# Sliding-window attention with an expert layer on one core: the inner tiles' global transposes set right behind the local ones, and global probabilities issued behind local ones

## The chip, the cores and the metric

The kernel runs on one NeuronCore of a Trainium2 chip. The metric is the time of one execution in device microseconds (us); the median of several runs counts. Engines are named as in the profile: PE (TensorE, with PEld for its weight loads), DVE (VectorE), ACT (ScalarE), POOL (GpSimd) and SP (SyncE, which issues all DMAs here). Each engine takes its instructions in the order of its own queue and waits on semaphores of the others.

## The reference

```python
B, H, Sl, D = q_l.shape            # 8, 8, 512, 64; Sg = 32 global tokens
k_all = concat([k_g, k_l]); v_all = concat([v_g, v_l])
out_g = softmax(scale * q_g @ k_all.T) @ v_all          # global queries see every key
s_ll = where(abs(i - j) <= 32, scale * q_l @ k_l.T, -1e9)
out_l = softmax(concat([scale * q_l @ k_g.T, s_ll])) @ v_all
x = concat([out_g, out_l]) as 4608 tokens x 512
h = max(max(x @ w1, x @ w2), x @ w3)                    # 512 -> 768
return h @ w_out                                        # 768 -> 512
```

All in float32. Local queries see a window of 32 keys to either side and the 32 global keys; global queries see everything.

## The kernel before, in words

**Tiles and units.** Heads go in pairs: 8 batches x 4 pairs are 32 units, numbered p. The 512 local queries of a unit are cut into four tiles of 128, t = 0 to 3; tile number sl = 4p + t from tile 16 on (`ORDER` shuffles the first 16). A tile's window of keys is 192 or 224 wide. The two outer tiles of a unit (t = 0 and 3) are "mixed" from unit 8 on: their two heads' chunks of keys are packed into three blocks of 128 columns rather than four. "Inner" are t = 1 and 2.

**One pass of the main loop**, for tile sl, writes in this order: the transposes of tile sl + 1's probabilities (`trans`, L398, into the PSUM tile T; below this is the T group), some matmuls of the expert layer (`fill`), the scores of tile sl + 3 (`scores`, L367 into S), more `fill`, the product of tile sl with the values (`pv`, L464 into O), a piece of the next unit's global part, `fill`, the transpose of the global probabilities that go with tile sl + 1 (`transg`, L423 into S), `fill`, and loads and splits for later tiles. Nothing loops on the chip: all is written out. A scheduler then sets the order of each engine's queue from that text and the dependences; PE's queue follows the text closely, SP's is moved about.

**The expert layer** of batch b - 1 is a generator that `fill` draws from: 16 passes draw just the 288 matmul steps of one batch. From tile 32 on PE's gaps between attention steps are filled with it: L503 (x by w1, w2, w3) and L522 (by w_out), each with a moving width of 512 and accumulating in one of three PSUM buffers pm. Its first matmuls for a batch follow the T group of tile 33, 49, 65, 81, 97 or 113. Float32 is split into a high and a low part by a copy (L111 on ACT, L109 on DVE) and a subtraction (L103 on DVE or POOL), for q, k, v, the transposed probabilities pt, x and h alike.

**Local probabilities.** `scores` reduces and exponentiates a tile, POOL (or ACT or DVE) scales it by 1/sum (L124), and SP copies it from s into the tile prob (L385 for t = 1 and 2, L382 and L383 for the mixed ones), from which PE transposes.

**Global part of unit p.** In the passes with t = 0 and 1 of unit p - 1, `glob` computes the scores of the 64 global queries of two heads (L298, into S) and DVE and ACT bring them into sg, of which there is one buffer. In the pass with t = 2 `glob_soft` makes the softmax. From unit 8 on `glob_put` sends its six pieces (`GPUT`) from sg into the three blocks of probg: the pieces 0 and 3 (block 0) in that pass, the others (blocks 1 and 2) in the pass with t = 3. Piece 5 goes as two transfers (L338), the rest as one each (L335): seven issues, called puts below. A tile's global transpose takes one block: `GCH` gives block 0 to t = 0 and 2, block 1 to t = 1, block 2 to t = 3. For t = 3 it stands in the T group already (L401), for the others it is L423. From S it is cast into pt (ACT) and the rest subtracted (DVE). The tiles S (scores, global scores, global transposes) take turns in two PSUM buffers; T has one.

Of the kernel before, what the change touches and what calls it, by code (L numbers as in the profile page):

```python
# [21 lines left out]
NP = H // 2  # L22
# [36 lines left out]
def body(ctx, tc, kin, qin, vin, min_, win, out):  # L59
    nc = tc.nc  # L60
# [267 lines left out]
    def glob_put(p, which):  # L328
        if p >= B * NP:
            return  # L330
        s, g = pg[p][0], f32(pgt[p])
        for k in which:
            c0, n, i, h, d0 = GPUT[k]
            if k < 5 or p < 2 * NP:
                nc.sync.dma_start(out=g[64 * h:64 * h + 64, i, d0:d0 + n], in_=s[:, c0:c0 + n])  # L335
            else:
                for j in range(2):
                    nc.sync.dma_start(out=g[64:64 + SG, 2, 64 * j:64 * j + 64], in_=s[SG * j:SG * j + SG, 480:544])  # L338

    def scores(i):  # L340
        if i >= NS:
            return
        sl = ORDER[i]
        p, t = divmod(sl, 4)
        c0, n = WIN[t]

        ps = pm.tile([128, 512], F32, name="pm") if i < 8 else psS.tile([128, 512], F32, name="S")
        s = s4[:, i % 4]
        if i < EARLY:
            sc[i] = s  # L350
        else:
            if len(prob) < 2:
                prob.append(const.tile([128, 2, 256], F32R, name="prob", tag=f"prob{2 + len(prob)}"))
                pool.memset(f32(prob[-1]), 0.0)
            sc[i] = prob[i % 2]
        nm = small.tile([128, 2], F32, name="nm")
        z = small.tile([128, 2], F32, name="z")
        ze = z8[:, i % 4]
        ph = [ps[:, 0:224], ps[:, 224:448]]
        for j in range(2):  # L360
            if i in NATK:

                pe.matmul(ph[j][:, 0:n], lhsT=qraw[i][:, 128 * j:128 * j + 128], rhs=nat_k(p)[0][:, c0:c0 + n],  # L363
                          start=True, stop=True)
                continue
            for a in range(2):
                pe.matmul(ph[j][:, 0:n], lhsT=qs[i][:, a, 128 * j:128 * j + 128],  # L367
                          rhs=kst[p][:, j, c0:c0 + n], start=(a == 0), stop=(a == 1))
        for j in range(2):
            dve.tensor_tensor_reduce(out=s[:, j, 0:n], in0=ph[j][:, 0:n], in1=mask[:, (1, 0, 1, 0)[t], 32 * (t == 0):32 * (t == 0) + n],  # L370
                                     scale=-0.125, scalar=3.0e38, op0=ALU.add, op1=ALU.min, accum_out=nm[:, j:j + 1])
            act.activation(out=s[:, j, 0:n], in_=s[:, j, 0:n], func=AF.Exp, bias=nm[:, j:j + 1], scale=-1.0,  # L372
                           accum_out=ze[:, j, 0:1])
        dve.tensor_reduce(out=z, in_=ze, axis=AX.X, op=ALU.add)
        dve.reciprocal(out=z, in_=z)
        for j in range(2):
            times(s[:, j, 0:n], s[:, j, 0:n], z[:, j:j + 1])
        if i >= EARLY:
            d = f32(sc[i])
            if mixed(p, t):  # L380
                d = d.rearrange("p j x -> p (j x)")
                nc.sync.dma_start(out=d[:, 0:256].rearrange("p (j x) -> p j x", j=2), in_=s[:, :, 0:128])  # L382
                nc.sync.dma_start(out=d[:, 256:384].rearrange("p (j x) -> p j x", j=2), in_=s[:, :, 128:192])  # L383
            else:
                nc.sync.dma_start(out=d[:, :, 0:n], in_=s[:, :, 0:n])  # L385
        spend("d", 2 * (n * 1.04 + 220) + 440)
        spend("a", 2 * (n * 0.833 + 278))

    def trans(sl):
        if sl >= NS:  # L390
            return
        s = sc.pop(sl)
        ps = psT.tile([128, 512], F32, name="T")
        pr, one = (ps, ident) if sl < EARLY else (ps.bitcast(F32R), identr)
        m = 3 if mixed(*divmod(ORDER[sl], 4)) else 4
        s = s.rearrange("p j x -> p (j x)")
        for x in range(m):
            pe.transpose(pr[:, 128 * x:128 * x + 128], s[:, 128 * x:128 * x + 128], one)  # L398
        p, t = divmod(ORDER[sl], 4)
        if t == 3 and mixed(p, t):  # L400
            pe.transpose(pr[:, 384:512], pgt[p][:, 2], identr)  # L401
        src = ps.rearrange("p (x q) -> p x q", q=128)[:, 0:m]
        if sl < NAT:
            pt = pts[sl] = att.tile([128, 4, 160], F32, name="pt", tag="pt")
            copy(pt[:, 0:m, 0:128], src, True)
        else:
            pt = pts[sl] = att.tile([128, 4, 2, 160], F32R, name="pt", tag="pt")
            copy(pt[:, 0:m, 0, 0:128], src, True)
            sub(pt[:, 0:m, 1, 0:128], src, f32(pt)[:, 0:m, 0, 0:128], True)
        if t == 3 and mixed(p, t):  # L410
            transg(sl, ps[:, 384:512])

    def transg(sl, bank=None):
        if sl >= NS:
            return
        p, t = divmod(ORDER[sl], 4)
        if t == 3 and mixed(p, t) and bank is None:
            return
        pt = pts[sl]
        i, h, n = GCH[t]  # L420
        g = bank if bank is not None else psS.tile([128, 512], F32, name="S")
        if bank is None:
            pe.transpose((g if p < NP else g.bitcast(F32R))[:, 0:128], pgt[p][:, i], ident if p < NP else identr)  # L423
        if mixed(p, t):
            src = g[:, 0:SG + SG * n].rearrange("p (x g) -> p x g", g=SG)
            if sl < NAT:
                copy(pt[:, 0:n + 1, 128:160], src, True)
                return
            hi, lo = [pt[:, 0:n + 1, a, 128:160] for a in range(2)]
        else:  # L430
            src = g[:, 64 * h:64 * h + 64 * n].rearrange("p (c j g) -> p c j g", j=2, g=SG)
            if sl < NAT:
                copy(pt.rearrange("p (j c) q -> p c j q", c=2)[:, 0:n, :, 128:160], src, True)
                return
            v = pt.rearrange("p (j c) a q -> p c j a q", c=2)
            hi, lo = [v[:, 0:n, :, a, 128:160] for a in range(2)]
        copy(hi, src, True)
        sub(lo, src, f32(hi), True)
# [113 lines left out]
    def fill(n):  # L552
        if mm[0]:
            for _ in range(n):
                next(mm[0], None)
# [29 lines left out]
    for sl in range(NS):  # L585
        p, t = divmod(ORDER[sl], 4)
        b = p // NP
        settle(4500)
        if sl == 8:
            mm[0] = moe_local(0, 0, 256)  # L590
        elif sl == 16:
            mm[0] = chain(mm[0], moe_local(0, 256, 256))
        elif sl >= 32 and sl % 16 == 0:
            fill(400)
            mm[0] = moe_local(b - 1)
        n = (7, 6, 5, 9) if sl < 16 else (4, 4, 3, 7)
        trans(sl + 1)
        fill(n[0])
        next_scores(sl + 4 if sl < 12 else max(15, sl + 3))
        if sl >= 16:  # L600
            if t == 2:
                split_k(p + 2)
                load_k(p + 3)
        elif sl in (10, 14):
            load_k(sl // 4 + 2)
        elif sl == 15:
            load_k(6)
        fill(n[1])
        pv(sl)
        if sl < 8:  # L610
            if p < 3:
                if t == 0:
                    glob(p + 1, 0)
                    glob(p + 1, 1)
                else:
                    glob_soft(p + 1)
        elif sl < 16:
            if sl in (12, 13):
                glob(NP, sl - 12)
            elif sl == 14:  # L620
                glob_soft(NP)
        elif t <= 1:
            glob(p + 1, t)
        elif t == 2:
            glob_soft(p + 1)
            if p + 1 >= 2 * NP:
                glob_put(p + 1, (0, 3))
        elif p + 1 >= 2 * NP:
            glob_put(p + 1, (1, 2, 4, 5))
        fill(n[2])  # L630
        transg(sl + 1)
        fill(n[3])
        split_v(sl + 2)
        load_v(sl + 4)
        for _ in range(WS[sl] if sl < len(WS) else 0):
            weight_step()
        if sl < 8:
            if t == 1:
                xs.setdefault(0, []).append(split_x(xr[p][:, 0:2, 0:128]))
        elif sl < 16:  # L640
            if t == 3:
                split_x(xr[p][:, 2:4, 0:128], xs[0][p], 256)
        elif sl % 16 >= 12:
            q = b * NP + sl % 16 - 12
            xs.setdefault(b, []).append(split_x(xr[q][:, :, 0:128]))
# [60 lines left out]
```

## Time and profile before

| | |
|---|---|
| median of 3 runs | 834.85 us (832.93 to 837.02) |
| the profiled execution | 834.52 us, span 832.7 us, mean clock 0.994 |
| PE busy | 803.1 us (96%), 4620 matmuls |
| DVE, ACT, POOL busy | 511.4, 522.3, 513.2 us |
| DMA queue of SP | 93.56 MB, 37.2% of 16 engines |
| chain that ended last | PE 81% of the span |

How to read the rows: a timeline row is start in us from the span's beginning, duration, engine, line, operation, the program's names out<-in, shapes, and how many alike are merged (x4); in brackets the engine's idle time before it and what ended that. Matmuls are pipelined and their ends are modelled, so two rows of PE overlap; the time between two starts says more. A wait row is total time, number of waits and the longest. DMA rows on SP are the time of issuing; the landing is later.

### The profile page before, as it was taken

How to read it: one execution, taken by the hardware profiler on the slowest of the kernel's cores; microseconds unless marked ns; L12 is line 12 of the kernel's file. 1: busy time of each engine (PE TensorE's matmuls, PEld its weight loads, DVE VectorE, ACT ScalarE, POOL GpSimd, SP SyncE). 2: the span in 40 equal slices, each digit the busy share in tenths (PEclk: the TensorE clock that was granted, in tenths of full speed). 3: DMA queues.
4: the chain of work that ended last, by engine and by line, in shares of the span. 5: the costliest groups of instructions: out<-in, count | busy, mean ns of one | idle time of the engine just before them, and what ended most of it. 6: DMA issues, size and time to landing. Idle time of an engine off the chain costs nothing.

```text
span 832.7 us, 16036 instructions
## 1 busy us (share of the span) xinstructions
PE 803.1 (96%) x4620; PEld 680.7 (82%) x4620; DVE 511.4 (61%) x1789; ACT 522.3 (63%) x1495; POOL 513.2 (62%) x725
## 2 busy tenths in 40 slices
PE   7779899899999999999999999999999999999997
PEld 5469789878888888888888888878888888888896
DVE  3778744866776677766775766767666676411121
ACT  5788756777676767776676677776776666411111
POOL 4689836786677667867676676866776664311211
PEclk9999999999999999999999999999999999999999
DMA  7566544443344433343335333443335332100001
GB/s 251 174 221 221 186 148 122 132 133 110 110 115 129 117 104 112 100 149 104 103 106 165 111 96 102 125 127 99 105 93 165 115 86 57 59 13 0 26 26 26
DMA packets 106856, 94.58 MB, mean 114 GB/s; under 512 B 31888, under 2 KB 95248, under 8 KB 106768
## 3 DMA queue, kind: packets, MB, share of 16 engines
q1 hardware_dynamic: 106768, 93.56, 37.2%
q8 instruction: 37, 0.61, 0.3%
q14 instruction: 51, 0.42, 0.2%
HBM read 56.85 MB, written 8.91 MB: 79 GB/s over the span
## 4 chain that ended last, share of the span: by engine, by line
PE 81%; DVE 2%; DMA 1%; issue 1%; ACT 1%; POOL 1%; POOLq 0%; DVEq 0%; ACTq 0%
PE pm L503 48%; PE pm L522 15%; PE O L464 6%; PE S L367 5%; PE T L398 3%; PE S L298 2%; DMA prob<-s 1%; PE S L363 1%; PE O L457 1%; PE S L423 1%; ACT s L372 0%; DMA probg<-sg 0%; DVE s L370 0%; PE T L401 0%; DMA qraw<-q_in 0%
## 5 line engine op out<-in xcount | busy, mean ns | idle before, releaser
L503 PE MATMUL pm<-xs,wh 128*128 128x512 f32 (+1 forms) x1440 | 421.8, 368 | 5.5 <-ACT xs L111 2.4
L503 PEld LDWEIGHTS pm<-xs,wh 128*128 128x128 f32 x1440 | 253.3, 189 | 36.6 <-ACT xs L111 2.9
L503 PE MATMUL pm<-xs,wl 128*128 128x512 f32 (+1 forms) x720 | 264.1, 367 | 1.0 <-POOL wl L177 1.0
L503 PEld LDWEIGHTS pm<-xs,wl 128*128 128x128 f32 x720 | 136.3, 189 | 20.9 <-issue 1.6
L124 POOL TENSOR_SCALAR s<-s,z 128x224 f32<-128x224 f32 (+1 forms) x244 | 104.0, 438 | 67.7 <-ACT lox L111 38.7
L522 PE MATMUL pm<-woh,h 128*128 128x512 f32 x408 | 133.4, 398 | 0.9 <-POOL h L103 0.9
L372 ACT ACTIVATE s<-s,nm 128x224 f32<-128x224 f32 (+1 forms) x256 | 118.0, 462 | 19.2 <-DVE nm L370 18.0
L103 POOL TENSOR_TENSOR h<-m,h 128x512 fp32r<-128x512 f32 (+1 forms) x60 | 68.3, 1138 | 98.4 <-ACT h L111 98.2
L511 DVE TENSOR_TENSOR m<-pm,m 128x512 f32<-128x512 f32 (+1 forms) x120 | 72.9, 608 | 71.1 <-PE pm L503 70.7
L103 DVE TENSOR_TENSOR pt<-T,pt 128x512 fp32r<-128x512 f32 (+2 forms) x126 | 70.2, 557 | 72.1 <-ACT pt L111 71.7
L103 POOL TENSOR_TENSOR qs<-qraw,qs 128x256 fp32r<-128x256 f32 x100 | 73.0, 738 | 57.0 <-ACT qs L111 41.9
L370 DVE CUSTOM_DVE_ANT_0 s<-S,mask 128x224 f32<-128x224 f32 (+1 forms) x240 | 80.5, 369 | 28.3 <-PE S L363 17.0
L522 PEld LDWEIGHTS pm<-woh,h 128*128 128x128 f32 x408 | 74.5, 188 | 14.0 <-POOL h L103 1.7
L111 ACT CAST pt<-T 128x512 fp32r<-128x512 f32 (+2 forms) x117 | 55.6, 476 | 48.1 <-PE T L398 41.9
L522 PE MATMUL pm<-wol,h 128*128 128x512 f32 x204 | 81.8, 401 | 1.2 <-POOL wol L177 1.2
L103 POOL TENSOR_TENSOR kst<-kraw,kst 64x576 fp32r<-64x576 f32 x50 | 71.6, 1431 | 14.0 <-DVE nm L370 7.9
L103 POOL TENSOR_TENSOR vs<-vraw,vs 128x256 fp32r<-128x256 f32 x102 | 75.5, 740 | 6.4 <-ACT vs L111 4.8
L464 PEld LDWEIGHTS O<-pt,vs 128*128 128x128 f32 x408 | 66.0, 188 | 8.6
L464 PE MATMUL O<-pt,vs 128*128 128x320 f32 (+1 forms) x408 | 72.8, 300 | 0.0
L111 ACT CAST qs<-qraw 128x256 fp32r<-128x256 f32 x99 | 40.2, 407 | 48.4 <-PE S L367 45.9
L367 PEld LDWEIGHTS S<-kst,qs 128*128 128x128 f32 x400 | 59.6, 190 | 9.1 <-DVE nmg L302 0.6
L111 ACT CAST h<-m 128x512 fp32r<-128x512 f32 (+1 forms) x60 | 33.4, 556 | 53.3 <-DVE m L511 53.3
(99 smaller groups left out, 1228.2 us busy)
## 6 DMA issues: line engine op xcount, KB each, us to landing
vraw<-v_in SPq DMA_DIRECT2D x64, 256.0 KB, 3.2
qraw<-q_in SPq DMA_DIRECT2D x100, 128.0 KB, 2.2
prob<-s SPq DMA_DIRECT2D x56, 224.0 KB, 2.4
wraw<-w_in SPq DMA_DIRECT2D x24, 512.0 KB, 3.6
out_dram<-o SPq DMA_DIRECT2D x32, 256.0 KB, 2.6
kraw<-k_in SPq DMA_DIRECT2D x25, 320.0 KB, 3.4
prob<-s SPq DMA_DIRECT2D x48, 128.0 KB, 2.2
prob<-s SPq DMA_DIRECT2D x48, 64.0 KB, 2.0
```

Of the source, the lines that this page charges most:

```text
L103: (dve if least(c) == "d" else pool).tensor_tensor(out=out, in0=a, in1=b, op=ALU.subtract)
L111: act.copy(out=out, in_=a)
L124: pool.tensor_scalar(out=out, in0=a, scalar1=col, scalar2=1.0, op0=ALU.mult, op1=ALU.mult)
L298: pe.matmul(ps[:, 0:n], lhsT=qgz.rearrange("p j x -> p (j x)")[:, 128 * j:128 * j + 128], rhs=kst[p][:, j, c0:c0 + n], start=(j == 0), sto ...
L367: pe.matmul(ph[j][:, 0:n], lhsT=qs[i][:, a, 128 * j:128 * j + 128], rhs=kst[p][:, j, c0:c0 + n], start=(a == 0), stop=(a == 1))
L370: dve.tensor_tensor_reduce(out=s[:, j, 0:n], in0=ph[j][:, 0:n], in1=mask[:, (1, 0, 1, 0)[t], 32 * (t == 0):32 * (t == 0) + n], scale=-0.12 ...
L372: act.activation(out=s[:, j, 0:n], in_=s[:, j, 0:n], func=AF.Exp, bias=nm[:, j:j + 1], scale=-1.0, accum_out=ze[:, j, 0:1])
L398: pe.transpose(pr[:, 128 * x:128 * x + 128], s[:, 128 * x:128 * x + 128], one)
L464: pe.matmul(o[:, j, 0:320].rearrange("p (a q) -> p a q", a=2)[:, :, 0:n], lhsT=vs[sl][:, 2 * j + c].rearrange("p a d -> p (a d)"), rhs=pt[ ...
L503: pe.matmul(ps[:, 0:n], lhsT=w[f][:, i, k], rhs=xs[k][:, a, c0:c0 + n], start=(q == 0), stop=(q == 11))
L511: dve.tensor_tensor(out=m[:, 0:n], in0=ps[:, 0:n], in1=m[:, 0:n], op=ALU.max)
L522: pe.matmul(ps, lhsT=hh[f][:, a, 128 * t:128 * t + 128], rhs=w[:, f], start=(q == 0), stop=(q == 17))
```

## The change

From tile 33 on the global transposes of inner tiles are written right behind the tile's T group. In the units from 8 on the puts of blocks 1 and 2 are written earlier, one issue fewer (pieces 1 and 4 go as one transfer), and tied on SP behind the local transfer written last: pieces 1 + 4 and 2 behind that of t = 1, piece 5 behind that of t = 2. No computation is added or left out.

```diff
@@ glob_put
         for k in which:
             c0, n, i, h, d0 = GPUT[k]
+            if k == 1 and p >= 2 * NP:
+                nc.sync.dma_start(out=g[0:64, 1:3, 32:128], in_=s[:, 0:512].rearrange("p (i x) -> p i x", i=2)[:, :, 128:224])
+                continue
@@ scores
-                nc.sync.dma_start(out=d[:, 256:384].rearrange("p (j x) -> p j x", j=2), in_=s[:, :, 128:192])
+                sent[0] = nc.sync.dma_start(out=d[:, 256:384].rearrange("p (j x) -> p j x", j=2), in_=s[:, :, 128:192])
             else:
-                nc.sync.dma_start(out=d[:, :, 0:n], in_=s[:, :, 0:n])
+                sent[0] = nc.sync.dma_start(out=d[:, :, 0:n], in_=s[:, :, 0:n])
@@ main loop
         trans(sl + 1)
+        inner = sl + 1 >= 32 and (sl + 1) % 4 in (1, 2)
+        if inner:
+            transg(sl + 1)
         fill(n[0])
...
             if p + 1 >= 2 * NP:
                 glob_put(p + 1, (0, 3))
+                with tc.issue_after(sent[0].ins):
+                    glob_put(p + 1, (1, 2))
         elif p + 1 >= 2 * NP:
-            glob_put(p + 1, (1, 2, 4, 5))
+            with tc.issue_after(sent[0].ins):
+                glob_put(p + 1, (5,))
         fill(n[2])
-        transg(sl + 1)
+        if not inner:
+            transg(sl + 1)
```

PE's queue at tile 33, where the expert layer of a batch begins. T group, scores (S from qs), O, the global scores (S from qgz), expert matmuls, and in the last third the lone global transpose. Before:

```order
L398 MATMUL T<-identr,prob 128x128 x4
L503 MATMUL pm<-xs,wh_98 128x512 x2
L503 MATMUL pm<-xs,wl_104 128x512
L503 MATMUL pm<-xs,wh_98 128x512
L367 MATMUL S<-kst,qs 128x192 x4
...
L298 MATMUL S<-kst,qgz 128x384 x2
L503 MATMUL pm<-xs,wl_104 128x512
L503 MATMUL pm<-xs,wh_98 128x512 x2
L423 MATMUL S<-identr,probg 128x128
L503 MATMUL pm<-xs,wl_104 128x512
L503 MATMUL pm<-xs,wh_98 128x512 x2
```

After, with the changed kernel's line numbers (five higher in this part):

```order
L403 MATMUL T<-identr,prob 128x128 x4
L428 MATMUL S<-identr,probg 128x128
L508 MATMUL pm<-xs,wh_98 128x512 x2
L508 MATMUL pm<-xs,wl_104 128x512
L508 MATMUL pm<-xs,wh_98 128x512
L372 MATMUL S<-kst,qs 128x192 x4
...
L298 MATMUL S<-kst,qgz 128x384 x2
L508 MATMUL pm<-xs,wl_104 128x512
L508 MATMUL pm<-xs,wh_98 128x512 x2
L508 MATMUL pm<-xs,wl_104 128x512
```

The global transpose has moved past eleven expert matmuls, the scores, O and the global scores, to the end of the T group; the same for each inner tile up to 126.

SP's queue around the transfers of unit 24, whose tile 97 begins a batch's expert layer. The transfer prob<-s of 2x224 is that of t = 1, the second one that of t = 2. Before:

```order
L335 DMA probg<-sg 64x128
L335 DMA probg<-sg 64x64
L335 DMA probg<-sg 64x96 x3
L338 DMA probg<-sg 32x64 x2
L260 DMA qraw<-q_in 128x256
L385 DMA prob<-s_94 128x2x224
L536 DMA out_dram<-o 128x512
L260 DMA qraw<-q_in 128x256
L272 DMA vraw<-v_in 128x2x256
L385 DMA prob<-s_94 128x2x224
L536 DMA out_dram<-o 128x512
```

After:

```order
L338 DMA probg<-sg 64x128
L338 DMA probg<-sg 64x64
L260 DMA qraw<-q_in 128x256
L390 DMA prob<-s_94 128x2x224
L335 DMA probg<-sg 64x2x96
L338 DMA probg<-sg 64x96
L541 DMA out_dram<-o 128x512
L260 DMA qraw<-q_in 128x256
L272 DMA vraw<-v_in 128x2x256
L390 DMA prob<-s_94 128x2x224
L341 DMA probg<-sg 32x64 x2
L541 DMA out_dram<-o 128x512
```

Five puts have left the place ahead of the first local transfer; as four issues, two follow it and two follow the second one. On ACT and DVE the moved transposes' casts and subtractions stand right behind those of the T group; POOL's queue is the same as before.

More of the change, by code (lines that the diff above doesn't have):

```diff
@@ L338, in glob_put @@
                     nc.sync.dma_start(out=g[64:64 + SG, 2, 64 * j:64 * j + 64], in_=s[SG * j:SG * j + SG, 480:544])
+    sent = [None]
     def scores(i):
```

## The prediction

> **What bounds the kernel now.** The page's first section, then the stretches of one batch each (the 16 local tiles beside one batch's expert layer), then the waits of TensorE. Stretch rows give the length, then busy us of PE, PEld, DVE, ACT and POOL, clock, DMA share and GB/s.
>
> ```profile
> PE 803.1 (96%) x4620; PEld 680.7 (82%) x4620; DVE 511.4 (61%) x1789; ACT 522.3 (63%) x1495; POOL 513.2 (62%) x725
> ...
> 266.00:358.00 92.00, 92.00 (x507) 78.16 (x507) 64.67 (x229) 65.43 (x188) 64.49 (x89) 1.00 0.40 116
> 450.00:542.00 92.00, 91.46 (x504) 77.52 (x503) 63.75 (x223) 64.71 (x187) 64.19 (x89) 1.00 0.39 115
> 542.00:634.00 92.00, 90.86 (x498) 76.70 (x497) 62.51 (x225) 64.54 (x187) 64.46 (x89) 1.00 0.39 115
> ```
>
> From tile 33 on PE has no idle time in most batches, at the full clock, and the others have about 30% to spare. So only two things can move the end: what a matmul costs PE, and the few places where PE stands still. The largest wait of PE that the profile finds between 174 and 728 us is this (total, times, longest):
>
> ```profile
> PE T L398 <- DMA prob<-s: 1.7, 2, 1.1
> ```
>
> The modelled ends of matmuls hide stalls below some 0.2 us, so I go by starts from here on (timeline rows: start, us, engine, line, operation).
>
> **Part 1: the 48 transposes that move on PE.** Tiles 33 to 126 with t = 1 or 2 are 48. Before, each one's global transpose (L423) stands alone among 512-wide matmuls.
>
> ```profile
> 371.07 0.63 PE L503 MATMUL pm<-xs,wh 128*128 128x512 f32 x2
> 371.54 0.22 PE L423 MATMUL S<-identr,probg 128*128 128x128 f32 x1
> 371.59 0.45 PE L503 MATMUL pm<-xs,wl 128*128 128x512 f32 x1
> 371.88 0.39 PE L503 MATMUL pm<-xs,wh 128*128 128x512 f32 x1
> ```
>
> In 371.88 - 371.07 = 0.81 us lie three 512-wide matmuls and the transpose. What three cost without it, from the chain of waits, where ten in a row take 2.27:
>
> ```profile
> 376.61 2.27 PE pm L503 x10
> ```
>
> 3 x 0.227 = 0.68, so the lone transpose costs 0.13 us. The row shows how: the next matmul starts 0.05 behind it, but the one after that 0.29 later rather than 0.23. In a group it costs what a fourth local transpose adds to three, since a fifth never occurs before. A group of four, and one of three, each up to the third long matmul behind it:
>
> ```profile
> 367.38 0.45 PE L398 MATMUL T<-identr,prob 128*128 128x128 f32 x4
> 367.68 0.69 PE L503 MATMUL pm<-xs,wh 128*128 128x512 f32 x2
> 368.21 0.39 PE L503 MATMUL pm<-xs,wl 128*128 128x512 f32 x1
> ...
> 447.44 0.37 PE L398 MATMUL T<-identr,prob 128*128 128x128 f32 x3
> 447.64 0.70 PE L522 MATMUL pm<-woh,h 128*128 128x512 f32 x2
> 448.18 0.40 PE L522 MATMUL pm<-wol,h 128*128 128x512 f32 x1
> ```
>
> 0.83 against 0.74: 0.09. The move saves 0.13 - 0.09 = 0.04 us per tile, 48 x 0.04 = 1.9 us. From above, a fifth cannot be cheaper than the 0.05 after which the next matmul starts behind a lone one (saving 3.8); from below it costs its whole weight load, uncovered:
>
> ```profile
> 371.31 0.14 PEld L423 LDWEIGHTS S<-identr,probg 128*128 128x128 f32 x1
> ```
>
> 0.13 - 0.14 = -0.01 each, 0.5 us lost. I take 1.9, because the fourth is the same operation in the same place. The Trainium skill (TensorE: Matmul & The Clock Gate, section Back-to-back issue gap) gives about 56 ns for an isolated 128-wide matmul and about 81 ns in a stream of weight loads and matmuls; by it the move would cost 48 x 0.025 = 1.2 us, an estimate. The 0.09 above agrees with its 81, the 0.13 does not agree with its 56, so the rows decide for a gain.
>
> **Part 2: the stalls at the first matmuls of a batch's expert layer.** The tile behind which a batch's layer begins (33, 49, 65, 81, 97, 113) has t = 1. Its T group waits for its own probabilities at four of these six. Last long matmul before the group, and the group:
>
> ```profile
> 177.74 0.40 PE L522 MATMUL pm<-wol,h 128*128 128x512 f32 x1
> 178.14 0.51 PE L398 MATMUL T<-identr,prob 128*128 128x128 f32 x4
> ...
> 452.79 0.39 PE L522 MATMUL pm<-wol,h 128*128 128x512 f32 x1
> 453.71 0.51 PE L398 MATMUL T<-identr,prob 128*128 128x128 f32 x4 [0.54 <-DMA prob<-s]
> ...
> 545.17 0.39 PE L522 MATMUL pm<-wol,h 128*128 128x512 f32 x1
> 546.69 0.51 PE L398 MATMUL T<-identr,prob 128*128 128x128 f32 x4 [1.14 <-DMA prob<-s]
> 547.04 0.69 PE L503 MATMUL pm<-xs,wh 128*128 128x512 f32 x2
> ...
> 638.41 0.40 PE L522 MATMUL pm<-wol,h 128*128 128x512 f32 x1
> 639.00 0.51 PE L398 MATMUL T<-identr,prob 128*128 128x128 f32 x4 [0.20 <-DVE xs L109]
> ```
>
> Less the ordinary 0.23 each: 0.17 + 0.69 + 1.29 + 0.36 = 2.5 us, and 0.05 more behind each (after a stall the group takes 0.35 to the next matmul, against 0.30 above): 2.7 us. Why tile 97 is late, from SP's queue, POOL's timeline and the chain of waits:
>
> ```profile
> 538.75 3.10 SPq L335 DMA_DIRECT2D probg<-sg  x5
> 541.89 1.22 SPq L338 DMA_DIRECT2D probg<-sg  x2
> 543.22 0.53 SPq L260 DMA_DIRECT2D qraw<-q_in  x1
> 543.85 0.68 SPq L385 DMA_DIRECT2D prob<-s  x1
> ...
> 539.54 0.88 POOL L124 TENSOR_SCALAR s<-s,z 128x224 f32<-128x224 f32 x2
> ...
> 543.85 2.71 DMA prob<-s
> ```
>
> The probabilities are ready at 540.42, but seven global issues stand ahead, back to back. After, two do (1.2 of the 4.3 us): puts until 540.0, the query load 0.6, and the local issue at 540.6, 3.2 us earlier. Landed 2.71 later, at 543.3, it is there 2.1 us before 545.4, when PE would come. The three smaller stalls need 0.2 to 0.7, so they go too. I take all 2.7; the other end is 0, if something right behind is late instead. Three candidates:
> - The moved transposes of t = 1 need the two probg transfers that now follow the local one: 540.6 + 0.7 + 0.7 (the new two-piece transfer, taken as the two-piece local one) = 542.0 for the second issue. Over all of L335's transfers:
>
> ```profile
> DMA to landing us min/median/max: 1.7/2.2/4.7
> ```
>
>   So it lands at 544.2, against 545.7 for the fifth transpose: 1.5 us of cover, of which a slow landing (4.7) takes all. Tile 33, the earliest stall, has least cover; I give it 0.05 us.
> - S has two buffers. The scores of the global part (L298) now wait until the transpose moved ahead of them is copied out, where they waited for an older one. The same unit's rows:
>
> ```profile
> 547.24 0.59 ACT L111 CAST pt<-T 128x512 fp32r<-128x512 f32 x1 [1.06 <-PE T L398]
> 547.85 0.69 DVE L103 TENSOR_TENSOR pt<-T,pt 128x512 fp32r<-128x512 f32 x1 [2.10 <-ACT pt L111]
> 549.93 0.33 PE L298 MATMUL S<-kst,qgz 128*128 128x384 f32 x1
> ```
>
>   DVE ends the local subtraction at 548.54; the moved global one, a quarter as wide at most and so under 0.4 by the local's 0.69, follows at once; the buffer is free by some 549.0 and 0.9 us of cover are left. Cost nothing; if DVE came 0.9 later, each further 0.1 would be 0.1 on PE.
> - The tile t = 3 before a batch's end is late for another reason, POOL, and is not helped. Its second transfer and its group:
>
> ```profile
> 532.42 0.59 SPq L383 DMA_DIRECT2D prob<-s  x1
> 534.32 0.40 PE L398 MATMUL T<-identr,prob 128*128 128x128 f32 x3
> ...
> DMA to landing us min/median/max: 2.0/2.0/4.3
> ```
>
>   It lands at about 534.4, when PE is there. POOL's order does not change, so what PE has saved in the two moved transposes just ahead (0.08) it may wait here again, at the five batch ends: 0.4 us given back.
>
> The other edits go together. One issue fewer per unit (the two 64x96 pieces become one): 24 x some 0.6 us of SP; what that moves is the local transfer behind it, counted in part 2, so nothing of its own. The last two puts (L338) move behind the local transfer of t = 2, one issue earlier than PE's need of them a tile later (some 6 us); the next unit's global scores refill sg, which has one buffer, after them. That transfer stood here in SP's queue:
>
> ```profile
> 546.27 0.66 SPq L385 DMA_DIRECT2D prob<-s  x1
> ```
>
> With three issues fewer ahead (1.9 us) it goes at about 544.4, the last put at 545.7, landed at 547.9, before L298 comes at 549.93 - 1.3 = 548.6. Cover 0.7 us; what is late then is a copy on ACT, not PE. Loads of queries and values pass the puts by 1.2 us or less; they are fetched two tiles ahead. Nothing.
>
> **Sum.** -1.9 - 2.7 + 0.05 + 0.4 = -4.15 us. The profiled execution took 834.52 us (span 832.7), 0.3 below the median of 834.85, well inside the runs' own spread (832.93 to 837.02). 834.5 - 4.2 = 830.3 us. About 0.5% (4.2 us) is what a measurement of this kernel can tell from no change, so the forecast lies on that line.
>
> **Rivals.**
> - Packing gains nothing (a fifth transpose costs its 0.14 load), the stalls go: -2.7 + 0.5 = 832.3 us. For it: PEld is busy 85% of these stretches. Against it: the fourth costs 0.09. Chance 0.13. With its 56 and 81 in place of the rows the Trainium skill (TensorE: Matmul & The Clock Gate, section Back-to-back issue gap) would give 834.5 - 2.7 + 1.2 = 833.0, an estimate; the row of 0.13 disagrees.
> - The stalls only change their cause. At each boundary the expert layer begins with data of its own (the casts of xs on DVE in the row at 639.00), and the transposes' puts land behind the local transfer; if one of them takes the whole 2.7, only part 1 is left: 834.5 - 1.9 = 832.6. For it: the row at 639.00 names xs. Against it: that stall ends with a start 0.6 after the last matmul at a place where the queue rows are as at 543.85. Chance 0.17.
> - Slower: the fifth transpose waits for its puts. PE takes its matmuls in order, so what is late there holds everything behind it, in all 24 units rather than at four. It decides from 4.2 / 24 = 0.17 us per unit on. The cover of 1.5 us is gone with landings of 3.7 rather than 2.2; landings of 4.2 would cost 24 x 0.5 = 12 and give 834.5 - 4.2 + 12 = 842 us. For it: 4.7 has been seen. Against it: the median is 2.2, and the puts now go ahead of the store to out_dram. Chance 0.08.
> - The change does nothing at all, 834.5: the order of instructions shows both moves made; 0.02.
>
> **How the numbers follow.** The forecast, both gains, has 0.60: 830.3, between 827.8 (part 1 at 3.8, nothing given back) and 831.7 (half of the stalls stay). The range from 827.8 to 834.6 takes in the first two rivals and the last, and leaves out the slow one and what lies below, together some 0.12. Faster by over 0.5%: the half of the forecast's case that lies below 830.5, and part 1's upper end, say 0.48; within 0.5%: the rest of it, the first two rivals and the last, 0.45; slower by over 0.5%: 0.07.
>
> **What would show it.** In the profile after: the group of five (T x4 and S x1) to the third long matmul behind it in 0.92 us; no wait of T for prob<-s at the batches' begins; three of them with the ordinary 0.23 before T; the local transfer of t = 1 issued some 3 us earlier against T. Wrong would make it: idle time before the S transposes with DMA probg<-sg as its end, waits of L298 for DVE or ACT pt, or 0.97 us and more per group of five.

## The result, and the profile after

| | before | after |
|---|---|---|
| median | 834.24 us of 6 runs (832.93 to 837.02) | 828.35 us of 6 runs (828.06 to 829.76) |
| profiled execution, its span | 834.52, 832.7 us | 828.59, 826.8 us |

The ratio is 0.9928, with a 95% interval from 0.9913 to 0.9944: faster by 0.56 to 0.87%. In a later set of five runs (experiment "the change again") the ratio was 0.9932, from 0.9918 to 0.9947; one of these five took 2700.81 us, for a reason that no trace shows, and is left out of the ratio. The forecast was 830.3 us, between 827.8 and 834.6. 828.35 lies inside that range, 2.0 us below the forecast.

The page's first section, and the stretches of one batch that were shown before (the same columns):

```profile
PE 799.3 (97%) x4620; PEld 681.8 (82%) x4620; DVE 512.6 (62%) x1789; ACT 520.8 (63%) x1495; POOL 513.6 (62%) x725
...
266.00:358.00 92.00, 91.97 (x509) 78.45 (x508) 64.81 (x229) 65.49 (x190) 64.53 (x89) 1.00 0.39 115
450.00:542.00 92.00, 92.00 (x509) 78.64 (x508) 64.42 (x229) 64.97 (x188) 65.03 (x90) 1.00 0.40 117
542.00:634.00 92.00, 92.00 (x511) 78.60 (x509) 65.11 (x229) 64.90 (x188) 64.50 (x89) 1.00 0.40 116
```

PE was busy for 90.86 of the 92 us of the last stretch before, and now for all 92: that is the stall of tile 97. The stretches also hold more matmuls (511 where 498 stood, 509 where 507 stood in a stretch without a stall), so the same work is done in less time. PE's busy time over the whole fell from 803.1 to 799.3 us with the same 4620 matmuls. That is not packing alone: with only the move it is 801.5 us, and with only the puts 801.3.

The T group of tile 97, from PE's timeline after:

```profile
542.17 0.39 PE L527 MATMUL pm<-wol,h 128*128 128x512 f32 x1
542.40 0.46 PE L403 MATMUL T<-identr,prob 128*128 128x128 f32 x4
542.70 0.25 PE L428 MATMUL S<-identr,probg 128*128 128x128 f32 x1
542.78 0.70 PE L508 MATMUL pm<-xs,wh 128*128 128x512 f32 x2
543.32 0.39 PE L508 MATMUL pm<-xs,wl 128*128 128x512 f32 x1
...
545.67 0.51 PE L298 MATMUL S<-kst,qgz 128*128 128x384 f32 x2
```

0.23 us now lie between the last long matmul and the group, where 1.52 lay before. From the group's start to the third long matmul behind it there are 543.32 - 542.40 = 0.92 us, against 0.83 for a group of four: the fifth transpose costs 0.09, as the fourth did. SP's queue at the same place, after:

```profile
534.79 1.14 SPq L338 DMA_DIRECT2D probg<-sg  x2
536.03 0.54 SPq L260 DMA_DIRECT2D qraw<-q_in  x1
537.51 0.63 SPq L390 DMA_DIRECT2D prob<-s  x1
538.24 0.62 SPq L335 DMA_DIRECT2D probg<-sg  x1
538.91 0.61 SPq L338 DMA_DIRECT2D probg<-sg  x1
```

The local issue stands 542.40 - 537.51 = 4.9 us ahead of its T group; before, it stood 546.69 - 543.85 = 2.8 us ahead. SP even waits between the query load and this issue (536.57 to 537.51), until POOL has scaled the probabilities: the queue is no longer what sets its time. Between tiles 32 and 127 no wait of T, S or L298 on PE is left in the records.

To see where the time went, I take the start of tile 32's T group and that of tile 127's as marks. Timelines of PE, before and then after:

```profile
172.38 0.37 PE L398 MATMUL T<-identr,prob 128*128 128x128 f32 x3
...
718.54 0.38 PE L398 MATMUL T<-identr,prob 128*128 128x128 f32 x3
```

```profile
171.48 0.37 PE L403 MATMUL T<-identr,prob 128*128 128x128 f32 x3
...
712.86 0.37 PE L403 MATMUL T<-identr,prob 128*128 128x128 f32 x3
```

The stage between the marks fell from 546.17 to 541.38 us, by 4.8. The rest behind tile 127 lost 0.2 (spans less marks: 114.16 and 113.94). Ahead of tile 32 it lost 0.9, where the change moves hardly anything; the experiment "the change again" shows that this is chance.

### The profile page after: what moved, and what is told of

Read it like the earlier page. It is cut to its first block, busy times and chain, and to the rows that moved or that the text cites. A ratio compares the mean times of both kernels' runs of the same rounds, so it can differ in the third digit from the quotient of the medians.

```text
span 826.8 us, 15905 instructions
## 1 busy us (share of the span) xinstructions
PE 799.3 (97%) x4620; PEld 681.8 (82%) x4620; DVE 512.6 (62%) x1789; ACT 520.8 (63%) x1495; POOL 513.6 (62%) x725
## 4 chain that ended last, share of the span: by engine, by line
PE 84%; DVE 1%; DMA 1%; POOL 0%; issue 0%; ACT 0%; POOLq 0%; DVEq 0%; ACTq 0%
PE pm L508 48%; PE pm L527 16%; PE O L469 6%; PE S L372 5%; PE T L403 4%; PE S L298 2%; PE O L462 1%; PE S L428 1%; PE S L368 1%; DMA prob<-s 1%; PE T L406 0%; DVE kst L109 0%; PE S L294 0%; ACT s L377 0%; POOL xs L103 0%
```

## The experiments

Three theories stood against each other. A: packing and puts each give a part, and the two add. B: the puts gain next to nothing, since the stalls change their cause. C: packing gains nothing. For each run two figures are given: the median against that of the kernel before on the same chip, and the length of the stage from tile 32 to tile 127 in its profile.

**The kernel before, again.** No edit; it shows how far two executions of one kernel differ.

> The kernel before, unchanged, once more with a profile. The traces of before and after differ by 0.9 us already at the T group of tile 32 (172.38 and 171.48 us), ahead of everything that the change touches on PE. If that is chance between executions, this one starts its T group of tile 32 anywhere from 171 to 173.5 us; if it belongs to the kernel before, again at 172.3 to 172.5. In both cases the stalls at tiles 81, 97 and 113 are there again, though each of another size.

The run took 835.85 us, and its stage 547.46 us, 1.3 more than the first one's. PE's waits between 172 and 728 us, in total, times and longest:

```profile
PE T L398 <- DMA prob<-s: 2.6, 4, 1.3
```

In the first profile these were 1.7 in 2. By starts, the T groups stand for 3.8 us beyond the ordinary 0.23 here and for 2.5 there, and in part at other tiles (34, 49, 97 and 113 differ by 0.4 to 1.1). Long stalls belong to this kernel, but where they fall and how long they are changes from one execution to the next. Tile 32 began at 172.56 us here and at 172.38 in the first profile, which by itself decides neither way.

**The move alone.** Only the transposes move; the puts stay as before.

```diff
         trans(sl + 1)
+        inner = sl + 1 >= 32 and (sl + 1) % 4 in (1, 2)
+        if inner:
+            transg(sl + 1)
 ...
-        transg(sl + 1)
+        if not inner:
+            transg(sl + 1)
```

> Only the transposes on PE are moved; the puts stand where they stood. Two independent gains: 48 transposes x 0.055 us (by the starts in the trace after) = 2.6 us less, the stalls at the first matmuls of a batch stay or grow by 0.1 each, so about 831.8 us against 834.2. Rival, the queue of SP is all: no change, 834.2. Rival, the transposes now ahead of their old place wait for their puts: idle time before the S transposes, slower than before.

Median 831.83 us of 9 runs against 834.32, ratio 0.9974 (0.996 to 0.9989). Stage 544.43 us: 1.7 below the first profile of before, 3.0 below the second. The stalls are still there, 2.7 us in all. PE's waits, and one of them in the timeline:

```profile
PE T L398 <- DMA prob<-s: 1.8, 4, 0.8
```

```profile
451.00 0.39 PE L522 MATMUL pm<-wol,h 128*128 128x512 f32 x1
452.23 0.51 PE L398 MATMUL T<-identr,prob 128*128 128x128 f32 x4 [0.85 <-DMA prob<-s]
452.58 0.25 PE L423 MATMUL S<-identr,probg 128*128 128x128 f32 x1
```

Tile 81 waits 1.0 us beyond the ordinary; then the group of five follows. No wait of the moved transposes for their puts is in the records. So packing gains by itself, and C falls. Against the first profile it is 1.7 + 0.2 (stalls longer by that much) + 0.2 (tiles t = 3 late by that much more) = 2.1 us, 0.044 for each of 48. Against the second it comes out nearly the same: 3.0 - 1.1 (stalls shorter) + 0.1 = 2.0.

**The puts alone.** The change without the move.

> Only the puts are moved and merged; the transposes stand alone, where they stood. Two independent gains: the stalls of 2.7 us go, some 0.2 comes back at the tiles t = 3 before a batch's end, so about 831.7 us against 834.2, and no wait of T for prob at tiles 81, 97, 113. Rival, packing is all: 834.2. Rival, the stalls only change their cause (xs): T of 81 and 97 is still 0.5 us or more behind the last matmul.

Median 830.81 us of 8 runs, ratio 0.9961 (0.9946 to 0.9976). Stage 543.58 us, 2.6 below the first profile and 3.9 below the second. No wait of PE is left in the stage. Tile 81 here:

```profile
449.11 0.22 PE L428 MATMUL S<-identr,probg 128*128 128x128 f32 x1
449.17 0.44 PE L527 MATMUL pm<-wol,h 128*128 128x512 f32 x1
...
450.61 0.39 PE L527 MATMUL pm<-wol,h 128*128 128x512 f32 x1
450.84 0.46 PE L403 MATMUL T<-identr,prob 128*128 128x128 f32 x4
451.13 0.69 PE L508 MATMUL pm<-xs,wh 128*128 128x512 f32 x2
```

0.23 us before the group, and a long matmul right behind it: the stall is gone without the move, nothing took its place at this tile, and B falls. The first row is the lone transpose of the tile before (t = 0). The two parts add as far as can be told: by medians -2.5 and -3.5 make -6.0, and the whole change measured -5.9; by stages against the first profile of before -1.7 and -2.6 make -4.3, and the whole change measured -4.8.

**All puts late.** This was to test the slow rival: pieces 1 + 4, 2 and 5 all go behind the local transfer of t = 2, one tile later than in the change.

```diff
                 glob_put(p + 1, (0, 3))
-                with tc.issue_after(sent[0].ins):
-                    glob_put(p + 1, (1, 2))
 ...
             with tc.issue_after(sent[0].ins):
-                glob_put(p + 1, (5,))
+                glob_put(p + 1, (1, 2, 5))
```

> As the change, but the puts of block 1 follow the local transfer of t = 2 rather than that of t = 1. If the moved transpose really takes part in PE's order with its wait, it stands some 2.2 us in each of 24 units (two issues and a landing behind a transfer that goes out at the time of its T group): about 828.4 + 50 = 878 us, with that idle time before the S transposes. If PE can go on past it, or the landing is quicker than the 2.2 us of the median, below 850 us.

One run took 840.33 us, far below the 878 expected; its stage is 553.72. The timeline of PE shows why:

```profile
339.72 0.46 PE L403 MATMUL T<-identr,prob 128*128 128x128 f32 x4
340.01 0.69 PE L527 MATMUL pm<-woh,h 128*128 128x512 f32 x2
...
341.47 0.62 PE L527 MATMUL pm<-woh,h 128*128 128x512 f32 x2
342.31 0.25 PE L428 MATMUL S<-identr,probg 128*128 128x128 f32 x1 [0.22 <-DMA probg<-sg]
342.40 0.66 PE L372 MATMUL S<-kst,qs 128*128 128x192 f32 x4
```

The scheduler took the transpose of t = 1 out of the T group and set it 2.6 us later, right ahead of the scores, presumably because its puts come late. So this kernel tests less than it was made for. It still has PE waiting for the puts:

```profile
PE S L428 <- DMA probg<-sg: 4.1, 15, 0.5
PE S L298 <- DVE pt L103: 1.0, 5, 0.2
```

That is the sign the prediction named for the slow case. The stage is 553.72 - 541.38 = 12.3 us longer than with the change, 0.51 per unit, three times the 0.17 from which that rival would have decided. By starts, 9.0 us of it lie right before the 24 transposes of t = 1. Late puts can thus turn the change into a loss; what they cost where the group of five stays together wasn't tried.

**The change again.** No edit.

> The change as it is, beside the next three: 828.4 us, 6 us under the kernel before. If the 1 us by which it was ahead before tile 32 was chance, its T group of tile 32 starts elsewhere this time, within 170 to 173 us.

Median 828.82 us of 5 runs against 834.75, ratio 0.9932; stage 541.50, within 0.1 of the first profile after. Tile 32's T group starts at 172.40 us here, 0.9 later than in the first profile after, and at the same place as before (172.38). So the 0.9 us ahead of tile 32 was chance.

**Relief for POOL, one head on DVE.** With the puts early, the tile t = 3 before a batch's end is late by more than before (next section). This takes its scaling by 1/sum from POOL: one head goes to ACT, one to DVE.

```diff
+        if off and e == "p":
+            e = off
 ...
-            times(s[:, j, 0:n], s[:, j, 0:n], z[:, j:j + 1])
+            times(s[:, j, 0:n], s[:, j, 0:n], z[:, j:j + 1], off="ad"[j] if i >= 32 and i % 16 == 15 else None)
```

> The change, and in addition the local probabilities of the tiles t = 3 at a batch's end (47, 63, 79, 95, 111, 127) are scaled on ACT and DVE, one head each, where POOL scales both otherwise. If what the change gives back is POOL's lateness, the five groups there take 0.83 us to the third long matmul behind instead of 0.95 to 1.05: 0.85 us less in all, about 827.5. Rival, those groups wait for the transfers of the global part (L406) or for DMA rather than for POOL: still 0.95 to 1.05, 828.4.

Median 831.04 us of 6 runs, ratio 0.9954 (0.9938 to 0.997); stage 543.09, 1.7 longer than with the change. The lateness at t = 3 is gone, but a new wait of PE is there. PE's waits, and then the timeline with POOL's, DVE's and PE's rows at one of the three places:

```profile
PE S L374 <- DVE nmg L304: 1.8, 3, 0.6
```

```profile
435.40 2.92 POOL L103 TENSOR_TENSOR kst<-kraw,kst 64x576 fp32r<-64x576 f32 x2
...
435.46 1.49 DVE L122 TENSOR_SCALAR s<-s,z 128x192 f32<-128x192 f32 x1
436.88 0.64 DVE L479 TENSOR_TENSOR xr<-O,lox 64x160 f32<-64x160 f32 x2
437.55 0.55 DVE L304 CUSTOM_DVE_ANT_0 sg<-S,sg 64x384 f32<-64x384 f32 x1
...
438.16 0.69 PE L374 MATMUL S<-kst,qs 128*128 128x192 f32 x4 [0.61 <-DVE nmg L304]
```

The scaling took DVE 1.49 us. The pass that empties S (L304) came that much later, and the scores that need this buffer of S waited. S has two buffers, so what DVE is late by reaches PE soon.

**Relief for POOL, both heads on ACT.** The same edit with off="a".

> The change, and the probabilities of the tiles t = 3 at a batch's end scaled on ACT, both heads. With one head on DVE the scaling of 128x192 took 1.49 us and not 0.60 where it ran beside POOL's subtraction of kst, and three scores waited for DVE behind it. If that was the cause of the loss there, none of those waits is left: from tile 32 to tile 127 540.5 us (541.4 less the 0.9 given back), 827.5 us in all. Rival, the order that the other scaling brings about costs it, whatever the engine: 543 again, 830 us.

Median 828.13 us of 6 runs against 834.36, ratio 0.9929 (0.9912 to 0.9946); stage 540.60, 0.8 to 0.9 below that of the change, against 540.5 expected. No wait of PE is left in the stage, and the five groups at t = 3 take 0.82 to 0.83 us. The lateness at t = 3 cost 0.8 us, then; the median cannot tell this from the change.

**The transposes of t = 0 too.** On top of the change, the global transpose of a tile t = 0 goes behind the T group of the tile t = 1 that follows, with that tile's own, into one S tile: a group of six.

```diff
         if inner:
-            transg(sl + 1)
+            if t == 0:
+                pair = psS.tile([128, 512], F32, name="S")
+                for q in range(2):
+                    pe.transpose(pair.bitcast(F32R)[:, 128 * q:128 * q + 128], pgt[p][:, q], identr)
+                transg(sl, pair[:, 0:128])
+                transg(sl + 1, pair[:, 128:256])
+            else:
+                transg(sl + 1)
 ...
-        if not inner:
+        if not inner and not (sl + 1 >= 32 and (sl + 1) % 4 == 0):
             transg(sl + 1)
```

> The change, and in addition the global transposes of the tiles t = 0 from tile 32 on leave their place and stand behind the T group of the next tile, t = 1, together with that tile's own: 24 lone transposes fewer. By what a lone one cost more than one in a group, 0.055 us by the starts, 1.3 us less: 827.1 (by the prediction's 0.04, 827.4). Rival, its copy comes too late for the product with the values in the same pass, or the two copies hold up DVE's work on the next scores: idle time before O or S, 0.2 us in 24 units, 833.

Median 827.75 us of 5 runs, ratio 0.9923 (0.9908 to 0.9938); stage 540.87, 0.5 below that of the change, where 1.3 was expected. The tiles t = 3 give back 1.2 us here against 0.9, so part of the gain was lost there once more; the rest of the difference is not explained.

**Both, first with one head on DVE, then with both on ACT.**

> The two additions together: 828.4 - 0.85 - 1.3 = 826.2 us if they are independent; if one takes the cover of the other, no better than the better of the two.

> The same scaling on ACT, together with the global transposes of t = 0 behind the T group of t = 1. With one head on DVE this took 539.8 us from tile 32 to tile 127. If DVE's part cost nothing there, 539.8 again and 827 us; if it held something up, up to 0.5 less.

With DVE: 827.32 us of 4 runs against 834.75, ratio 0.9915 (0.9901 to 0.9929), stage 539.77; in this order of DVE the new wait did not arise. With ACT: 826.25 us of 4 runs against 834.36, ratio 0.9901 (0.9887 to 0.9916), stage 540.01. That is the fastest of all, some 2 us below the change; its interval still touches that of the first comparison (0.9913). The group of six at tile 81 in it:

```profile
450.49 0.46 PE L405 MATMUL T<-identr,prob 128*128 128x128 f32 x4
450.78 0.34 PE L610 MATMUL S<-identr,probg 128*128 128x128 f32 x2
450.96 0.70 PE L510 MATMUL pm<-xs,wh 128*128 128x512 f32 x2
451.49 0.40 PE L510 MATMUL pm<-xs,wl 128*128 128x512 f32 x1
```

451.49 - 450.49 = 1.00 us: the sixth costs 0.08.

## Why the prediction was right, point by point

**Part 1, the 48 transposes that move on PE: right, a little small.** The group of five takes 0.92 us to the third long matmul, as forecast, so the choice of the fourth transpose as the nearest row was right. The saving was 2.1 us in the move alone (worked out above), and 543.58 - 541.38 = 2.2 from the puts alone to the whole change, 2.4 with the 0.2 that the tiles t = 3 gave back more. That is 0.044 to 0.05 each where 0.04 was taken, or 0.2 to 0.5 us too little in all; two executions of one kernel differ by 0.1 to 1.3 us in this stage, so the runs do not show where that lies. The Trainium skill (TensorE: Matmul & The Clock Gate, section Back-to-back issue gap) gives some 81 ns for a 128-wide matmul in a stream, and the fifth and sixth agree with 0.08 to 0.09 us. Its 56 ns for an isolated one, of which it says itself that no weight load is counted in, is no price for a lone one among 512-wide matmuls, as the prediction's estimates took it: that cost 0.13 us here, and the move alone gained.

**Part 2, the stalls at the first matmuls of a batch's expert layer: right in kind, under-sized.** All went, and neither the fifth transposes nor the casts of xs took their place. The puts alone shortened the stage by 2.6 to 3.9 us, depending on which profile of before they are held against; the forecast has 2.7 for them, since its 0.05 and 0.4 belong to the moved transposes. Held against the profile from which the 2.7 was read, 2.6 remained although the tiles t = 3 took back 0.56, so 3.1 was gained. The rest is that 2.7 was read off one execution, and the next had stalls of 3.8, in part in other places. The step "the local transfer of t = 1 issued some 3 us earlier" held: before, the issue stood 545.4 - 543.85 = 1.55 us ahead of the time at which PE would have come, and now 4.9, which is 3.3 earlier.

**The give-back at the tile t = 3 before a batch's end: right in place, too small, and for another reason.** From the group's start to the third long matmul a group of four took 0.83 us before. Tile 95 after, from the timeline, with POOL's, SP's and PE's rows:

```profile
524.76 2.92 POOL L103 TENSOR_TENSOR kst<-kraw,kst 64x576 fp32r<-64x576 f32 x2
527.78 0.83 POOL L124 TENSOR_SCALAR s<-s,z 128x192 f32<-128x192 f32 x2
...
529.39 0.65 SPq L388 DMA_DIRECT2D prob<-s  x1
...
531.20 0.56 PE L403 MATMUL T<-identr,prob 128*128 128x128 f32 x3
531.59 0.25 PE L406 MATMUL T<-identr,probg 128*128 128x128 f32 x1
531.67 0.69 PE L527 MATMUL pm<-woh,h 128*128 128x512 f32 x2
532.20 0.39 PE L527 MATMUL pm<-wol,h 128*128 128x512 f32 x1
```

532.20 - 531.20 = 1.00 us, so 0.17 is lost. The chain reads backwards: POOL scales at 527.78, behind two subtractions of k; the second transfer goes at 529.39 and PE comes for it 1.8 us later. The five places sum to 0.86 us; they held 0.12 in the first profile before, so 0.74 is new, against 0.4 forecast. The step that failed is "what PE has saved in the two moved transposes just ahead", 0.08 each: the puts alone, with no transpose moved, already give 0.68 (0.56 new), and the move alone only 0.2 more than before. So what returns here comes mostly from the removed stalls: POOL's work does not come earlier by as much as PE does. The prediction priced part 2 without this, as if its gain could be kept whole. Taking the scaling from POOL brought back 0.8 us, which shows that POOL is the cause.

**The sum.** By the first two profiles -4.8 us in the stage (-2.6 puts, -2.2 the move) against -4.15 forecast. By the second profile of before it would be -6.1, and the medians say -5.9. So the forecast was 0.6 to 2 us short: 0.2 to 0.5 lies in part 1, and the stalls of before were 1.3 us larger in the second profile than in the one it was read from. The range's lower end of 827.8 does not follow from its terms, which give 834.5 - 3.8 - 2.7 = 828.0; the measured 828.35 lies above both. How much of the medians' 5.9 each part holds to a tenth stays open, since stalls and the time ahead of tile 32 both wander by 1 us or more between executions.

**The rivals.** "Packing gains nothing" fell with the move alone, "the stalls only change their cause" with the puts alone. The slow one did not arise: at tile 97 the merged put goes 542.70 - 538.24 = 4.5 us ahead of the fifth transpose and the one behind it 3.8; the merged ones landed after 2.0 us in the median and 3.8 at most, and PE has no wait for a put in the records. With later puts its sign appeared.

## What to carry to other kernels

Small matmuls that stood alone among long ones cost more here than in a row (0.13 against 0.09 us); count what a fourth adds to three, and see whether the data is there in time. On an in-order queue of transfers it is the position that counts: what PE needs next goes first, and several small issues that are needed later go behind it. When a stall is removed, look for the next thing that was only just in time (here POOL's scaling), and price it by the whole gain and not by the last step; and profile the kernel before twice, since stalls move between executions.

## What the runs showed of the hardware

**DVE waits while POOL works.** In the kernel with one head on DVE the scaling of 128x192 there took 0.30 us at one place (at 344.17, where one instruction of POOL ends at 344.18 and its next begins at 344.26) and 1.49 at another (435.46, shown above). In the slow case POOL had begun the first of two subtractions 0.06 us earlier; these two take 2.92, so the first ends at about 436.9, and DVE at 436.95. In the kernel with the group of six and one head on DVE, from the timeline:

```profile
431.15 1.52 POOL L103 TENSOR_TENSOR h<-m,h 128x512 fp32r<-128x512 f32 x1
...
432.18 0.60 DVE L122 TENSOR_SCALAR s<-s,z 128x192 f32<-128x192 f32 x1
```

POOL ends at 432.67, DVE 0.1 later, at 432.78. These two kernels hold twelve such scalings on DVE from tile 47 on. Eleven of them took 0.57 to 1.49 us and ended 0.11 to 0.12 us behind the POOL instruction beside which they had begun, whether that had 0.45 or 1.38 us left; the twelfth is the one at 344.17. So DVE's instruction seems to stand until POOL's is over. The Trainium skill (SBUF — State Buffer, section SBUF: two separate sides) says that the two engines share a pair of ports, which the one that starts first holds for its whole instruction, where DVE's instruction runs in a mode that uses two ports or has two inputs in SBUF. The rows agree with the waiting; no run here shows in which mode DVE ran, or takes POOL's instruction away at the same place.

**The start of the kernel wanders.** Tile 32's T group began between 170.28 us (the puts alone) and 173.83 (one head on DVE) in twelve profiles, although almost nothing ahead of it differs, and twice the same kernel differed by 0.2 (before) and by 0.9 us (after). A gain below 1 us is better measured as the length of a stage than by the end, if the stage has no stalls: it was 541.38 and 541.50 us in two profiles of the change, but 546.17 and 547.46 in two of the kernel before.
